# Attention's last rows on the whole TensorE array, and two small steps of other stages made on POOL

## The chip, the core and the metric

One core of a Trainium2 chip runs the whole program in one launch. The metric is device time in microseconds, the median of a few runs. TensorE (PE in the profile, with its weight loads as PEld) multiplies, VectorE (DVE), ScalarE (ACT) and GpSimd (POOL) do the elementwise work, and SyncE (SP) issues the DMAs.

## What is computed

Three layers follow each other: causal attention with a decay from the cumulated sums of `s`, an FFN whose activation is h cos h, and an RMS-normed gated FFN. The weights come as 64-bit floats.

```python
# attention: q, k, v (4, 8, 576, 64), s (4, 8, 576)
scores = q @ k.T / 8
cum = cumsum(maximum(s, 0))
bias = -(cum[:, None] - cum[None, :])
scores = where(causal, -1e9, scores + minimum(bias, 0))
attn = exp(scores - max(scores)); attn = attn / (sum(attn) + 1e-9)
x = attn @ v                      # -> (2304, 512)
# FFN 1: w_in (512, 2048), w_out (2048, 512)
h = x @ w_in;  x = (h * cos(h)) @ w_out
# FFN 2: w_gate, w_val (512, 1536), w_out (1536, 512)
xn = x / rms(x) * rms_g
out = (silu(xn @ w_gate) * (xn @ w_val)) @ w_out
```

## The kernel before

Attention works on 16 pairs of heads, one head in partitions 0 to 63, the other in 64 to 127. A pair's 576 rows are cut in parts: "a" (rows 0 to 255) and "b" (rows 256 to 575). Rows 256 to 383 and 384 to 511 are scored per head by `score` (L427, the product; L432, the decay added by another matmul). The last 64 rows of both heads share one tile of 128 partitions, called "p" (`score_p`): for each half of 288 keys, two matmuls of 64 contraction rows by 64 columns (L455) write head 0 to the upper and head 1 to the lower half of one PSUM bank, and one matmul over all 128 partitions (L456) adds the decay. A float32 matmul shows as two MATMULs in the trace, a transpose and a matmul of type fp32r as one. DVE adds the mask and takes the row minimum (L439, L459), ACT takes the exponential with its row sum `rs` (L467), `norm` makes 2 pi / (sum + 1e-9) as two small DVE steps (L475, L477) and scales the rows by it (L482 to L484, one of three engines). PE transposes the tiles against `ident` (L498), the result is copied to `P` (L284, L287), and `av` multiplies by V (L530): for part "b" five key tiles for two heads, the last of them 64 keys by the 64 last rows. V is padded with zeros to 640 rows and Q holds, behind row 512, the last rows of head 0 and of head 1 in columns of their own, with zeros in the other head's partitions.

FFN 1 runs 72 units of 24 + 12 matmuls (`gemm1` L630, `gemm2` L636), all of the full 128 x 128 shape, the first of them between attention's work. FFN 2 runs 72 units of 24 + 9 (the same lines, 384 columns a block). TensorE works in split single precision: each weight is a rounded part and its rest.

A weight chunk (`chunk`, 68 of them: 32 for FFN 1, 36 for FFN 2) is made from 64-bit floats, loaded to `raw` (3 buffers) as pairs of 32-bit words, the low word first. The high word times 2^-112 goes to `cv` (2 buffers) on POOL (L359) or ACT (L360). DVE then shifts it left by 3 (L362), adds the sign bit of the high word (L363) and the top 3 bits of the low word (L365). A copy (L284, L287 or L291) rounds it into the weight tile and a subtraction (L295 on DVE or L297 on POOL) makes the rest.

The order of all instructions of an engine is fixed when the program is built: `Plan.order` is a list scheduler that takes the ready step with the lowest due time on the engine that is free first, by the costs written beside each step, and, where a step may run on several engines, picks the one that its costs make earliest. An engine runs its list in order, so what stands at its head and waits holds up all behind it. A change of costs or of steps therefore moves others.

## Time and profile before

| | us |
|---|---|
| median of 3 runs | 1119.66 (1119.5 to 1120.15) |
| the profiled execution's own time | 1122.79 |
| its span, first to last instruction | 1121.0 |
| PE busy in it | 1091.6 |
| DVE, ACT, POOL busy | 567.0, 535.5, 139.8 |

Attention ends near 306 us. From there to about 600 us only FFN 1 runs, from about 600 to 716 us FFN 1's last units stand beside 30 of the weight chunks of FFN 2, and after that FFN 2 runs alone. The page's busy share of PE is not its share at full rate: the end of each matmul is modelled to overlap the next one's start, so a length of the timeline is to be read from start to next start. The granted clock of PE has two levels, 1.2 and 2.4 GHz. The page shows it at 7 tenths of the upper one in the first of its 40 slices and at 9 or more in all others; a window from 14 to 20 us has 0.50 of it, one from 612 to 616 us 0.83 and one from 616 to 620 us 0.75.

### The profile page before, as it was taken

The numbers are of one execution on the slowest core, as the hardware profiler recorded it, in microseconds if no ns is written. First come the engines' busy times: TensorE is split into PE (matmuls) and PEld (weight loads), VectorE is DVE, ScalarE is ACT, GpSimd is POOL, SyncE is SP. The second block draws the span as 40 slices with busy tenths as digits, with TensorE's granted clock in tenths as the row PEclk, the third lists the DMA queues.
The fourth block names the chain that finished last, engine by engine and source line by source line (L and its number), as shares of the span: only waits on it lengthen the run. The fifth ranks groups of instructions, "written<-read, shape, count | busy, mean of one in ns | idle before, by whom it ended". The sixth has DMA issues, their size and how long they took to land.

```text
span 1121.0 us, 16903 instructions
## 1 busy us (share of the span) xinstructions
PE 1091.6 (97%) x6538; PEld 933.7 (83%) x6538; DVE 567.0 (51%) x1296; ACT 535.5 (48%) x1113; POOL 139.8 (12%) x152
## 2 busy tenths in 40 slices
PE   8899999999999999999999899999999999999998
PEld 6457676676799999999998788899999999999997
DVE  7896999775464444534447989621221211211211
ACT  5889898998844444434435555321221211211111
POOL 3331244111020000000002332100000000000000
PEclk7999999999999999999999999999999999999999
DMA  6663676744293010000102446110010100100000
GB/s 197 226 203 127 214 271 220 228 133 135 77 379 115 19 38 20 20 23 16 38 20 78 157 118 208 56 57 1 3 55 1 57 1 1 43 1 1 29 1 29
DMA packets 51376, 101.27 MB, mean 90 GB/s; under 512 B 7520, under 2 KB 27488, under 8 KB 51296
## 3 DMA queue, kind: packets, MB, share of 16 engines
q1 hardware_dynamic: 51296, 100.19, 27.1%
q8 instruction: 51, 0.84, 0.3%
q14 instruction: 29, 0.24, 0.1%
HBM read 77.63 MB, written 22.54 MB: 89 GB/s over the span
## 4 chain that ended last, share of the span: by engine, by line
PE 54%; issue 25%; DVE 14%; DMA 3%; ACT 3%; POOL 1%; DVEq 0%; POOLq 0%; SPq 0%; ACTq 0%
PE bank L630 27%; PE bank L636 15%; PE bank L498 3%; PE bank L530 3%; DVE cv L363 3%; DVE cv L365 3%; PE bank L427 3%; DMA wr<-wo_d 2%; DVE cv L362 1%; DVE u L295 1%; DVE e L439 1%; PE bank L455 1%; PE bank L432 1%; DVE rn L475 1%; DMA raw<-in_w_gate_dram 1%
## 5 line engine op out<-in xcount | busy, mean ns | idle before, releaser
L636 PE MATMUL bank<-wr,g 128*128 128x512 f32 x996 | 248.6, 398 | 5.3 <-ACT g L284 5.3
L295 DVE TENSOR_TENSOR u<-bank,u 128x512 f32<-128x512 f32 (+1 forms) x144 | 89.8, 623 | 317.2 <-PE bank L630 238.9
L630 PE MATMUL bank<-xa,wi 128*128 128x256 f32 x1728 | 223.5, 284 | 1.6 <-DVE u L295 1.6
L630 PEld LDWEIGHTS bank<-xa,wi 128*128 128x128 f32 x1728 | 217.5, 191 | 8.4 <-DVE u L295 2.0
L636 PEld LDWEIGHTS bank<-wr,g 128*128 128x128 f32 x996 | 183.9, 190 | 42.9 <-ACT g L284 6.7
L284 ACT ACTIVATE g<-u 128x512 fp32r<-128x512 f32 (+1 forms) x131 | 75.4, 576 | 266.0 <-DVE u L295 266.0
L295 DVE TENSOR_TENSOR g<-u,g 128x512 fp32r<-128x512 f32 (+1 forms) x127 | 80.9, 637 | 70.0 <-ACT g L284 69.8
L630 PE MATMUL bank<-xb,wi 128*128 128x384 f32 x528 | 101.6, 337 | 0.0
L630 PEld LDWEIGHTS bank<-xb,wi 128*128 128x128 f32 x528 | 93.2, 188 | 1.6
L630 PE MATMUL bank<-xb,wr 128*128 128x384 f32 x480 | 92.5, 337 | 0.0
L295 DVE TENSOR_TENSOR u<-u,bank 128x512 f32<-128x512 int32 x72 | 49.4, 685 | 80.4 <-ACT u L740 79.2
L740 ACT ACTIVATE u<-bank,quarter 128x512 int32<-128x512 f32 x72 | 49.4, 686 | 83.7 <-PE bank L630 81.9
L630 PEld LDWEIGHTS bank<-xb,wr 128*128 128x128 f32 x480 | 85.1, 188 | 1.7
L467 ACT ACTIVATE e<-e,mn 128x128 f32<-128x128 f32 (+3 forms) x128 | 70.6, 555 | 13.9 <-DVE mn L439 13.5
L742 ACT ACTIVATE u<-u,half_pi 128x512 f32<-128x512 f32 x72 | 52.1, 724 | 38.5 <-DVE u L295 38.3
L636 PE MATMUL bank<-wi,g 128*128 128x512 f32 x270 | 67.0, 392 | 0.0
L822 ACT ACTIVATE u<-bank 128x384 f32<-128x384 f32 x72 | 35.3, 490 | 64.4 <-PE bank L630 56.3
L439 DVE CUSTOM_DVE_ANT_0 e<-bank,cm 128x128 f32<-128x128 f32 (+3 forms) x128 | 57.7, 484 | 15.4 <-PE bank L432 15.1
L636 PE MATMUL bank<-ws,g 128*128 128x512 f32 x246 | 64.5, 401 | 0.0
L359 POOL TENSOR_SCALAR cv<-raw 128x512 f32<-128x512 f32 x22 | 17.1, 777 | 348.2 <-DVE wi L295 277.6
L636 PEld LDWEIGHTS bank<-wi,g 128*128 128x128 f32 x270 | 50.3, 188 | 9.7 <-ACT g L284 0.3
L498 PE MATMUL bank<-ident,e 128*128 128x128 f32 x320 | 53.7, 287 | 3.9 <-DVE mn L439 3.4
(129 smaller groups left out, 1456.0 us busy)
## 6 DMA issues: line engine op xcount, KB each, us to landing
raw<-in_w_out_dram SPq DMA_DIRECT2D x28, 512.0 KB, 4.4
raw<-in_w_in_dram SPq DMA_DIRECT2D x16, 512.0 KB, 3.8
wo_d<-ws SPq DMA_DIRECT2D x16, 512.0 KB, 3.7
ws<-wo_d SPq DMA_DIRECT2D x16, 512.0 KB, 4.5
wr<-wo_d SPq DMA_DIRECT2D x16, 512.0 KB, 10.6
raw<-in_w_gate_dram SPq DMA_DIRECT2D x12, 512.0 KB, 3.8
raw<-in_w_val_dram SPq DMA_DIRECT2D x12, 512.0 KB, 3.7
qr<-in_q_dram SPq DMA_DIRECT2D x16, 320.0 KB, 4.5
```

The source lines that it names most:

```text
L284: alts.append(("ACT", (act_p if psum else act_s)(n), lambda: act.activation(o(), i(), AF.Copy, scale=scale)))
L295: alts = on("DVE", dve1(n), lambda: dve.tensor_tensor(out=o(), in0=a(), in1=b(), op=op))
L363: plan.op(on("DVE", dve1(512), lambda: dve.scalar_tensor_tensor(out=v(), in0=top(), scalar=-(2 ** 31), in1=v(), op0=ALU.bitwise_and, op1=A ...
L365: plan.op(on("DVE", dve1(512), lambda: dve.scalar_tensor_tensor(out=v(), in0=low(), scalar=29, in1=v(), op0=ALU.logical_shift_right, op1=A ...
L439: plan.op(on("DVE", dve1(w) + 17, lambda o=o, w=w, i=i, e=e: dve.tensor_tensor_reduce(out=Es[e]()[:, o:o + w], in0=Sp[e]()[:, o:o + w], in ...
L467: plan.op(on("ACT", act_s(w) + 187, lambda E=E, o=o, w=w, i=i: act.activation(E()[:, o:o + w], E()[:, o:o + w], AF.Exp, scale=-1.0, bias=s ...
L498: pe.transpose(tr()[:m, 128 * j:128 * j + 128], E[0]()[:, E[2] + c:E[2] + c + m], ident)
L630: pe.matmul(h, w[:, a, 128 * k:128 * k + 128], x[k // 2][:, k % 2, c, :blk], start=(n == 0), stop=(n == 11))
L636: pe.matmul(acc[t], g[a][:, 128 * t:128 * t + 128], w[:, c, :], start=(first and (a, c) == (0, 0)), stop=(last and (a, c) == (1, 0)))
L740: plan.op(on("ACT", act_p(512) + 93, lambda u=u, h=h: act.activation(u().bitcast(I32), h(), AF.Identity, bias=quarter)), [h], [u])
L742: plan.op(on("ACT", act_s(512) + 93, lambda u=u: act.activation(u(), u(), AF.Sin, scale=-TWO_PI, bias=half_pi)), [], [u], table="sin")
L822: plan.op(on("ACT", act_p(BLK2), lambda us=us, h=hs[0]: act.activation(us(), h()[:, :BLK2], AF.Silu)), [hs[0]], [u], table="silu")
```

## The change

Four edits, which leave the result what it was:

- `score_p` multiplies both heads at once. The Q columns 512 to 639 are block diagonal over the two heads, so one float32 matmul over 128 contraction rows and 128 columns gives what the two of 64 x 64 gave. Its cost in the plan falls.
- The tile "p" is 640 wide instead of 576, its 64 last columns are set to zero once by POOL, before the loads of `s`. The transpose of its last columns takes 128 instead of 64, the copy to `P` 128 partitions instead of 64, and the last key tile of `av` contracts over 128 rows, 64 of them zero.
- In `chunk`, POOL multiplies the high word in place by zero, which leaves its sign alone; DVE then ors the low word's top bits into it (L364 of the new code), and a second DVE step shifts `cv` by 3 and ors the two (L366). Three DVE steps become two, and a POOL step is added to each of the 68.
- The first small step of `norm` (L475, the sum plus 1e-9, times 2 pi) runs on POOL; 48 instructions leave DVE.

```diff
-           3: ring("e3", 2, [128, 512], F32, "att"), "p": ring("ep", 2, [128, S], F32, "att")}
+           3: ring("e3", 2, [128, 512], F32, "att"), "p": ring("ep", 2, [128, 640], F32, "att")}
...
-        plan.op(on("DVE", dve2(512), lambda: dve.tensor_scalar(out=v(), in0=v(), scalar1=3, scalar2=None, op0=ALU.logical_shift_left)), [], [g])
+
+        plan.op(on("POOL", pool1(512), lambda: pool.tensor_scalar(out=top().bitcast(F32), in0=top().bitcast(F32), scalar1=0.0, scalar2=1.0, op0=ALU.mult, op1=ALU.mult)), [], [raw])
         plan.op(on("DVE", dve1(512), lambda: dve.scalar_tensor_tensor(
-            out=v(), in0=top(), scalar=-(2 ** 31), in1=v(), op0=ALU.bitwise_and, op1=ALU.bitwise_or)), [raw], [g])
+            out=top(), in0=low(), scalar=29, in1=top(), op0=ALU.logical_shift_right, op1=ALU.bitwise_or)), [], [raw])
         plan.op(on("DVE", dve1(512), lambda: dve.scalar_tensor_tensor(
-            out=v(), in0=low(), scalar=29, in1=v(), op0=ALU.logical_shift_right, op1=ALU.bitwise_or)), [raw], [g])
+            out=v(), in0=v(), scalar=3, in1=top(), op0=ALU.logical_shift_left, op1=ALU.bitwise_or)), [raw], [g])
...
             def qk():
-                for e in range(2):
-                    hd, q0 = slice(64 * e, 64 * e + 64), 512 + 64 * e - run.qs.start
-                    pe.matmul(Sp()[hd, :288], run.q()[hd, q0:q0 + 64], run.k()[hd, gs], start=True, stop=False)
+                q0 = 512 - run.qs.start
+                pe.matmul(Sp()[:, :288], run.q()[:, q0:q0 + 128], run.k()[:, gs], start=True, stop=False)
                 pe.matmul(Sp()[:, :288], run.pk(), ds()[:, o + gs.start:o + gs.stop], start=False, stop=True)
-            plan.op(on("PE", 488 + 127 + 2 * SWITCH_PE, qk), [run.q, run.k, run.pk, (ds, o)], [Sp], rows=0.9)
+            plan.op(on("PE", 480 + 127 + SWITCH_PE, qk), [run.q, run.k, run.pk, (ds, o)], [Sp], rows=0.9)
...
-            plan.op(on("DVE", 204, lambda: dve.tensor_scalar(
+            plan.op(on("POOL", 204, lambda: pool.tensor_scalar(
...
-... + [("p", 512, 64)],
+... + [("p", 512, 128)],
...
-                out(lambda: P()[:64, 3, 0:64], lambda: tr()[:64, 384 + 64 * e:448 + 64 * e], 64)
+                out(lambda: P()[:, 3, 0:64], lambda: tr()[:, 384 + 64 * e:448 + 64 * e], 64)
...
-                    jobs.append((4, 64, 256, 320, [p[:64, 3, 0:64] for p in ps]))
+                    jobs.append((4, 128, 256, 320, [p[:, 3, 0:64] for p in ps]))
...
+    for b in (s_b, cum):
+        plan.op(on("POOL", 130, lambda b=b: pool.memset(b()[:, S:640], 0.0)), [], [(b, "pad")])
```

The plan is made anew from these steps. Over the whole program the built order differs in the counted steps above and in who takes a free step: of the subtractions that make a weight's rest POOL has 34 before and 26 now (L297), and DVE, which has 53 row scalings (L483) before, now has 70 plus 6 of "p" instead of 11.

PE, one pair in the middle of attention, where the profile of before shows 212 us. Before, two 64-row matmuls and L456 stand between transposes (L498):

```order
L498 MATMUL bank_152<-ident,e_169 128x128 x4
L455 MATMUL bank_149<-kr_156,qr_154 64x288 x2
L456 MATMUL bank_149<-ds_161,pk_158 128x288
L498 MATMUL bank_150<-ident,e_168 128x128 x4
L455 MATMUL bank_151<-kr_156,qr_154 64x288 x2
L456 MATMUL bank_151<-ds_161,pk_158 128x288
```

The same place of the change:

```order
L498 MATMUL bank_152<-ident,e_169 128x128 x4
L455 MATMUL bank_149<-kr_156,qr_154 128x288
L456 MATMUL bank_149<-ds_161,pk_158 128x288
L498 MATMUL bank_150<-ident,e_168 128x128 x4
L455 MATMUL bank_151<-kr_156,qr_154 128x288
L456 MATMUL bank_151<-ds_161,pk_158 128x288
```

The place stays between the same neighbours; two instructions of half shape became one of full shape. Of the 32 such places 29 stood behind a full-shape matmul, and 30 do now.

DVE in the later part of FFN 2's weight chunks. Before, a chunk is three steps (L362, L363, L365) and the subtraction (L295) that ends it, if POOL doesn't make that one; here the end of one chunk and the whole of the next, with a step of an FFN unit between:

```order
L295 TENSOR_TENSOR wr_3171<-cv_128,wr_3171 128x512
L362 TENSOR_SCALAR cv_129<-cv_129 128x512
L363 SCALAR_TENSOR_TENSOR cv_129<-raw_127,cv_129 128x512
L365 SCALAR_TENSOR_TENSOR cv_129<-raw_127,cv_129 128x512
L295 TENSOR_TENSOR u_132<-bank_152,u_132 128x384
L295 TENSOR_TENSOR wr_3175<-cv_129,wr_3175 128x512
```

The same part now:

```order
L295 TENSOR_TENSOR wr_3154<-cv_128,wr_3154 128x512
L364 SCALAR_TENSOR_TENSOR raw_126<-raw_126 128x512
L366 SCALAR_TENSOR_TENSOR cv_129<-cv_129,raw_126 128x512
L364 SCALAR_TENSOR_TENSOR raw_127<-raw_127 128x512
L295 TENSOR_TENSOR wr_3157<-cv_129,wr_3157 128x512
L366 SCALAR_TENSOR_TENSOR cv_128<-cv_128,raw_127 128x512
```

A chunk is two DVE steps, and the first of them reads what POOL made. POOL in that stretch before, between roundings (L291) and subtractions (L297):

```order
L291 TENSOR_SCALAR wi_115<-cv_129 128x512
L297 TENSOR_TENSOR wi_115<-cv_129,wi_115 128x512
L297 TENSOR_TENSOR wr_3142<-cv_128,wr_3142 128x512
L297 TENSOR_TENSOR wr_3156<-cv_128,wr_3156 128x512
L297 TENSOR_TENSOR wi_117<-cv_129,wi_117 128x512
```

and now, with the new sign step (L363) of each chunk between them:

```order
L363 TENSOR_SCALAR raw_127<-raw_127 128x512
L291 TENSOR_SCALAR wi_115<-cv_129 128x512
L297 TENSOR_TENSOR wi_115<-cv_129,wi_115 128x512
L363 TENSOR_SCALAR raw_125<-raw_125 128x512
L363 TENSOR_SCALAR raw_126<-raw_126 128x512
L297 TENSOR_TENSOR wr_3112<-cv_128,wr_3112 128x512
L363 TENSOR_SCALAR raw_127<-raw_127 128x512
```

The sign steps stand in one list with the rounding and the subtraction of earlier chunks, and a chunk's DVE steps come after its own.

## Rows read from the trace of the kernel before

**Rows 1.** The page, part 1: busy time, share of the span, instructions, of each engine.

```profile
PE 1091.6 (97%) x6538; PEld 933.7 (83%) x6538; DVE 567.0 (51%) x1296; ACT 535.5 (48%) x1113; POOL 139.8 (12%) x152
```

**Rows 2.** Four stretches: start:end, length, busy of PE, PEld, DVE, ACT, POOL; PEclk; DMA.

```profile
60.00:120.00 60.00, 59.13 (x424) 38.86 (x422) 46.93 (x149) 54.37 (x139) 13.79 (x18) 1.00 0.51 166
120.00:200.00 80.00, 76.83 (x528) 53.98 (x522) 77.38 (x194) 72.36 (x167) 32.35 (x34) 1.00 0.71 238
200.00:310.00 110.00, 109.90 (x784) 78.66 (x781) 64.46 (x217) 94.24 (x219) 12.98 (x16) 1.00 0.44 140
600.00:720.00 120.00, 109.85 (x604) 97.84 (x603) 107.46 (x177) 63.15 (x113) 40.91 (x34) 0.99 0.46 142
```

**Rows 3.** The chain that ended last, share of each stretch by line, same four stretches.

```profile
by line: PE bank L530 19.3%; PE bank L498 19.0%; PE bank L427 16.3%; PE bank L630 14.3%; PE bank L455 8.4%; PE bank L636 5.0%; PE bank L456 4.4%; PE bank L432 4.1%; DVE e L439 2.2%; DVE rn L475 1.9%; issue 1.8%; DVE cv L363 1.6%; DVE cv L36
...
by line: DVE cv L363 13.2%; DVE cv L365 13.1%; DVE e L439 8.7%; issue 7.5%; DMA raw<-in_w_out_dram 5.2%; DVE u L295 5.2%; DVE cv L362 4.5%; DVE e L483 4.1%; DVE rn L475 4.1%; DVE P L287 3.9%; PE bank L530 3.5%; DVE wi L295 2.4%; DVE ws L295
...
by line: PE bank L498 20.4%; PE bank L530 17.4%; PE bank L636 17.2%; PE bank L630 17.1%; PE bank L427 12.7%; PE bank L455 5.7%; PE bank L456 3.0%; PE bank L432 2.9%; PE bank L720 0.9%; DVE st L701 0.9%; ACT xo L696 0.6%; ACT P L284 0.4%; DV
...
by line: issue 221.4%; DVE cv L363 14.7%; DVE cv L365 13.4%; PE bank L630 12.6%; PE bank L636 10.7%; DVE cv L362 7.3%; DVE u L295 6.3%; DVE y L709 4.0%; DVE wr L295 2.9%; POOL wi L297 2.8%; ACT wr L284 2.6%; DVE wi L295 2.6%; DVE g L295 2.5
```

**Rows 4.** PE timeline around one score_p: start, length, engine, line, operation, shapes, count.

```profile
212.99 0.60 PE L498 MATMUL bank<-ident,e 128*128 128x128 f32 x4
213.52 0.70 PE L455 MATMUL bank<-kr,qr 64*64 64x288 f32 x4
214.16 0.40 PE L456 MATMUL bank<-ds,pk 128*128 128x288 f32 x1
214.39 1.00 PE L630 MATMUL bank<-xa,wi 128*128 128x256 f32 x7
```

**Rows 5.** PE timeline a little earlier: both PV steps and one transpose group.

```profile
197.67 2.45 PE L530 MATMUL bank<-P,vr 128*64 128x320 f32 x20 [0.22 <-ACT P L284]
200.05 0.55 PE L498 MATMUL bank<-ident,e 128*128 128x128 f32 x3
...
203.72 0.87 PE L530 MATMUL bank<-P,vr 128*64 128x256 f32 x8
204.52 1.66 PE L636 MATMUL bank<-ws,g 128*128 128x512 f32 x6
...
208.07 0.66 PE L498 MATMUL bank<-ident,ep 128*128 128x128 f32 x4
208.48 1.67 PE L630 MATMUL bank<-xa,wi 128*128 128x256 f32 x12
```

**Rows 6.** L362 alone in two of the stretches: start:end, length, DVE busy, count; PEclk; DMA.

```profile
120.00:200.00 80.00, 9.18 (x18) 1.00 0.71 238
600.00:720.00 120.00, 13.72 (x30) 0.99 0.46 142
```

**Rows 7.** Four lines on DVE and POOL: ns min/median/max of one, first and last start.

```profile
L362 DVE TENSOR_SCALAR cv<-cv x68: 412/421/1529, 15.5 to 712.8; 128x512 int32<-128x512 int32 x68
...
L475 DVE TENSOR_SCALAR rn<-rs x48: 150/170/1243, 14.1 to 297.0; 128x4 f32<-128x4 f32 x16, 128x3 f32<-128x3 f32 x16, 128x2 f32<-128x2 f32 x16
...
L359 POOL TENSOR_SCALAR cv<-raw x22: 644/670/1080, 28.5 to 657.6; 128x512 f32<-128x512 f32 x22
...
L297 POOL TENSOR_TENSOR wi<-cv,wi x18: 1267/1531/1764, 20.0 to 695.2; 128x512 fp32r<-128x512 f32 x18
```

**Rows 8.** Timelines near 600 us, DVE first, then POOL: start, length, line, operation.

```profile
599.92 0.55 DVE L295 TENSOR_TENSOR xc<-xr,xc 128x384 fp32r<-128x384 f32 x1
...
607.43 1.00 DVE L295 TENSOR_TENSOR xc<-xr,xc 128x384 fp32r<-128x384 f32 x1
...
610.03 1.25 DVE L704 SCALAR_TENSOR_TENSOR st<-st 128x2 f32<-128x2 f32 x1
...
607.04 0.97 POOL L359 TENSOR_SCALAR cv<-raw 128x512 f32<-128x512 f32 x1
609.85 1.41 POOL L297 TENSOR_TENSOR wi<-cv,wi 128x512 fp32r<-128x512 f32 x1 [1.83 <-ACT wi L284]
```

More of the change, by code (lines that the diff above doesn't have):

```diff
@@ L490, in tr @@
                 self.P[e] = p32_r.new()
-            srcs = {0: [((e, 0), 0, 128), ((e, 1), 0, 128), ((e, 1), 128, 128)], 1: [((e, 2), 128 * c, 128) for c in range(3)] + [("p", 512, 64)],
+            srcs = {0: [((e, 0), 0, 128), ((e, 1), 0, 128), ((e, 1), 128, 128)], 1: [((e, 2), 128 * c, 128) for c in range(3)] + [("p", 512, 128)],
                     2: [((e, 3), 128 * c, 128) for c in range(4)], 3: [("p", 128 * c, 128) for c in range(4)]}[i]
@@ L579, in attention_moe_moe @@
     s_b, cum = e_r["p"].new(), e_r["p"].new()
-    load(s_b, lambda: s, 294912, [], [s_b])
-    plan.op(on("DVE", dve2(S), lambda: dve.tensor_scalar(out=s_b(), in0=s_b(), scalar1=0.0, scalar2=None, op0=ALU.max)), [], [s_b])
+    for b in (s_b, cum):
+        plan.op(on("POOL", 130, lambda b=b: pool.memset(b()[:, S:640], 0.0)), [], [(b, "pad")])
+    load(lambda: s_b()[:, :S], lambda: s, 294912, [], [(s_b, 0)])
+    plan.op(on("DVE", dve2(S), lambda: dve.tensor_scalar(out=s_b()[:, :S], in0=s_b()[:, :S], scalar1=0.0, scalar2=None, op0=ALU.max)), [], [(s_b, 0)])
     plan.op(on("DVE", dve1(S), lambda: dve.tensor_tensor_scan(
-        out=cum(), data0=ones.to_broadcast([128, S]), data1=s_b(), initial=0.0, op0=ALU.mult, op1=ALU.add)), [s_b], [cum])
+        out=cum()[:, :S], data0=ones.to_broadcast([128, S]), data1=s_b()[:, :S], initial=0.0, op0=ALU.mult, op1=ALU.add)), [(s_b, 0)], [(cum, 0)])
     def less(b, o, w, mid, scale=8.0, **kw):
@@ L587, in less @@
         plan.op(on("DVE", dve2(w) + 61, lambda: dve.tensor_scalar(
-            out=b()[:, o:o + w], in0=cum()[:, :w], scalar1=c(), scalar2=scale, op0=ALU.subtract, op1=ALU.mult)), [cum], [(b, o)], **kw)
+            out=b()[:, o:o + w], in0=cum()[:, :w], scalar1=c(), scalar2=scale, op0=ALU.subtract, op1=ALU.mult)), [(cum, 0)], [(b, o)], **kw)
     for i, (t, mid) in enumerate(((0, 63), (1, 191), (2, 319), ("p", 543), (3, 447))):
```

## The prediction

> **What bounds the kernel now.** I read the busy times first, then the stretches, then the chain of waits in each, and last the timelines of the places that the change touches. PE is busy for 1091.6 of 1121.0 us [rows 1], but its busy time counts drains and overlaps, so the stretches say more. From 60 to 120 and from 200 to 310 us PE has next to no idle time (59.13 of 60, 109.90 of 110 us busy, [rows 2]) and the chain lies on PE's lines; L455 alone, the half-shape score of the last rows, holds 8.4% of the first (5.0 us) and 5.7% of the second (6.3 us) [rows 3]. These stretches are PE-led: a nanosecond less on PE there is one less in total. From 120 to 200 us DVE leads: 77.38 of 80 us busy [rows 2], with the weight chunks' lines L363, L365 and L362 and the small L475 on the chain [rows 3]; PE idles for 3 us. ACT, at 72.36 us, is close behind DVE. From 600 to 720 us DVE leads again (107.46 of 120 us, PE 109.85), and L362 is 7.3% of that stretch on the chain, 8.8 us [rows 2, 3]. The "issue" in that row is a wait that began long before the stretch. Elsewhere PE runs FFN units that the change doesn't touch.
>
> **The change part by part.** *The score on the full array.* From L455's start to the start of what follows L456 the trace has 213.52 to 214.39, 0.87 us [rows 4]. Entering the half shape costs too: four transposes take 0.53 us up to L455 (212.99 to 213.52) and 0.41 us up to a full-shape matmul (208.07 to 208.48) [rows 4, 5], so 0.12 us more. Together 0.99 us. The two heads already run side by side: four MATMULs of 288 columns take 0.64 us (213.52 to 214.16), two passes of 0.32 with their drain. The change makes two passes of 288 columns with the full shape. No float32 product of that shape and length is in attention; the nearest are the PV steps, two passes of 256 and two of 128 columns in 0.80 us (203.72 to 204.52), and 2432 columns of passes in 2.38 us (197.67 to 200.05) [rows 5], about 1.0 ns a column with all drains. So a pass is at most 0.30 us; with a drain of some 0.1 us taken off each PV step it is 0.25, which I take. L456 takes 0.23 us now (214.16 to 214.39) because its weights come behind a switch; twelve FFN matmuls of 256 columns take at most 1.67 us [rows 5], 0.14 each, so 288 columns in step take 0.15. After: 2 x 0.25 + 0.15 = 0.65 us, saving 0.34 a place; the bounds are 0.16 (0.30 a pass, L456 unchanged) and 0.38 (0.80 ns a column, so 0.23 a pass). Eighteen of the 32 places lie in the PE-led stretches (5.0 and 6.3 us of chain at 0.63 a place, eight and ten): **6.1 us**, from 2.9 to 6.8.
>
> The rows show two tiles side by side gaining nothing over one full pass: 0.32 us a pass against the 0.25 estimated. The Trainium skill's page "TensorEngine Tiling (Array Packing)", section "Theoretical Speedup", speaks against the edit: a small dimension of 64 or less promises up to 2x from tiles. Were that factor lost here, with passes of 0.50 us, a place would cost 1.15 us instead of 0.99, and the 18 places would lose 2.9 us instead of gaining 6.1. I don't expect it, since both heads fit in one pass.
>
> *The last PV tile and the transposes.* Part "b" has 1664 more columns of passes than part "a" and takes 1.58 us longer (2.38 against 0.80) [rows 5]. That is 0.95 ns a column with the switch in it; at 0.80 to 0.90 without, it is 0.08 to 0.25 us too much for the columns alone: its switch to the 64-row shape. I take 0.12, as the entry above. Ten of 16 part "b" steps are in PE-led stretches: **1.2 us** (0.8 to 2.5). Transposing 128 instead of 64 columns changes nothing: the spacing of transposes is 0.10 us [rows 5], and the copies to P have the same 64 columns on more partitions. The two memsets of the pads come before the loads and are hidden by the wait for `s`.
>
> *The weight chunks.* L362 goes, 421 ns alone [rows 7] and 0.51 us on average in the one DVE-led stretch (9.18 us for 18), 0.46 in the other (13.7 for 30) [rows 6]. What it holds of the chain is 3.6 us (4.5% of 80) and 8.8 us [rows 3]. Added is a POOL step like L359, 670 ns, up to 1080 [rows 7], which the chunk's first DVE step waits for; before, the chunks scaled on ACT needed no POOL at all. It costs DVE time as well: L295 on `xc` takes 0.55 us alone and 1.00 us when POOL's L359 runs beside it (607.43 against 607.04 to 608.01) [rows 8], 0.45 us lost to one POOL step. The other end is nothing, when DVE is idle or reads PSUM. I take 0.2, under the middle, because in the last third of FFN 2's chunks POOL has few subtractions and its sign steps run ahead of DVE. So the first stretch keeps 0.51 - 0.2 = 0.31 us of a 0.51 us step, the second 0.26 of 0.46: 2.2 of 3.6 us and 5.0 of 8.8.
>
> *L475 to POOL.* 48 DVE steps of 170 ns median [rows 7] go; on the chain they are 4.1% of 80 us, 3.3 us, and 1.1 us from 60 to 120 [rows 3]. DVE's L477 now waits for POOL, where a subtraction of 1531 ns [rows 7] may stand ahead. But before, L475 itself stood still beside such a subtraction (1243 ns at most, [rows 7]). I keep half of it where DVE leads, 1.6 us, and nothing elsewhere.
>
> These sum to 8.8 us. Against that stands the list order on POOL: a sign step behind a rounding and a subtraction waits 0.7 + 1.5 us, and DVE's L364 waits at the head of its list, with the h and g steps of an FFN unit queued behind it, and PE behind those. Of the weights' subtractions 26 stay on POOL; I charge two or three such waits, 2.8 us, and keep **6.0 us** (0 to 16). PE's own savings in these stretches count nothing while DVE leads.
>
> Sum: 6.1 + 1.2 + 6.0 = 13.3 us. The profiled execution took 1122.79 us, 1.8 over its span and 3.1 over the median; it would become 1109.5. From the median, 1119.66 - 13.3 gives **1106**.
>
> **The rivals.** *Both bounds fall.* If POOL's steps hide, DVE gives its 15.7 us (3.6, 8.8, 3.3), and in the DVE-led stretches PE, then next in line, has its 14 cheaper scores (4.8 us) to follow with. With 7.3 us from the PE-led ones at most 27.8 us, 1092; with some of it lost to ACT, 1095. For it: POOL is busy for a third of those stretches [rows 2]. Against: ACT is at 72 of 80 us.
>
> *PE's part alone.* The new POOL step and its waits eat all that DVE gained: 1119.66 - 7.3 = 1112.
>
> *Slower: POOL's step holds DVE.* If each sign step holds DVE for as long as the longer rows show, 0.97 us (607.04) [rows 8], the 48 chunks of the two DVE-led stretches lose 48 x (0.97 - 0.48) = 23.5 us, less 7.3: 1136. It decides from 0.48 + 7.3 / 48 = 0.63 us a chunk on; one step beside L359 lost 0.45, and a step of 2 columns beside a subtraction took 1.25 us (610.03) [rows 8], to the end of that one. For it: two POOL operations may follow each other. Against: L359 itself stretches to 1080 ns, so it is POOL that waits in part of the cases. The Trainium skill's page "SBUF — State Buffer", section "Who interferes with whom", has the rule behind this: of GpSimd and a VectorE step with two SBUF inputs the later one blocks until the first has ended. The rows at 607 and 610 us agree with it.
>
> *It doesn't do what it says.* If a full-shape pass with its weight load costs what the pair costs, and POOL eats the rest, the time stays, 1119.
>
> **How the numbers follow.** The forecast has 0.52 (1100 to 1111 alone), both bounds fall 0.20, PE's part alone 0.15, no effect 0.04, slower 0.09. The range leaves out the slower case, the no-effect case and the last of the lower one: 1094 to 1115. Faster by over 0.2% (2.2 us, about what a measurement here tells from nothing) is 0.52 + 0.20 + 0.15 = 0.87, same 0.04, slower 0.09.
>
> **What would show it.** In the trace of the changed kernel the step from the last transpose group to L456's successor should be some 0.35 us shorter, the stretch of pure attention work should end 6 to 12 us earlier, DVE's busy time from 600 to 720 us should fall by about 10 us, and POOL's total should rise by some 60 us (68 x 0.7 and 48 small ones). The prediction is wrong if DVE's L364 shows idle time behind POOL's L363 of more than 0.3 us a chunk, if L364 or L366 take much longer than L363 and L365 did, if the plan's new order puts an FFN unit behind a late chunk, or if PE loses its clock in a wait that wasn't there before.

## The result, and the profile after

The changed kernel takes 1110.26 us (1108.53 to 1112.65 in four runs, before 1119.91 beside it): 0.9913 of before, with a 95% interval of 0.9901 to 0.9925. That is 9.7 us less (8.4 to 11.1). The prediction said 1106, with a range of 1094 to 1115: the side and the range were right, and of the 13.3 us that it summed 9.7 came. The profiled execution took 1108.53 us, 1.7 under the median.

The page, busy times over the whole program (of before: [rows 1]):

```profile
PE 1078.3 (97%) x6474; PEld 938.8 (85%) x6474; DVE 547.5 (49%) x1209; ACT 529.0 (48%) x1098; POOL 186.3 (17%) x256
```

PE is 13.3 us shorter, DVE 19.5, and POOL 46.5 longer. A part of PE's 13.3 is its clock at the start (last section), so that it equals the prediction's sum is chance. The span fell by 14.2 us (1121.0 to 1106.8), so PE's idle time, where DVE's relief would show, hardly moved: 29.4 us before, 28.5 now. Four stretches, as in [rows 2] (start:end, length, busy of PE, PEld, DVE, ACT, POOL; granted clock; DMA). The last starts 10 us earlier than there, since the same work does:

```profile
60.00:120.00 60.00, 57.53 (x413) 42.92 (x410) 48.85 (x128) 52.43 (x125) 27.61 (x40) 1.00 0.60 198
120.00:200.00 80.00, 77.64 (x525) 56.09 (x525) 72.92 (x184) 72.25 (x167) 45.20 (x59) 1.00 0.70 231
200.00:310.00 110.00, 110.00 (x789) 86.50 (x788) 61.23 (x197) 90.92 (x211) 16.40 (x32) 1.00 0.50 165
590.00:710.00 120.00, 112.02 (x618) 100.63 (x617) 101.13 (x156) 62.84 (x111) 48.86 (x54) 0.99 0.46 142
```

From 200 to 310 us PE is as full as it was. From 60 to 120 us it now idles for 2.5 us instead of 0.9. In the last stretch DVE fell from 107.46 to 101.13 us of 120, yet PE gained only 2.2 us of work. The chain that ended last, by line, from 120 to 200 and from 590 to 710 us (of before: [rows 3]):

```profile
by line: PE bank L638 10.9%; PE bank L498 9.1%; issue 8.2%; PE bank L428 7.0%; DMA raw<-in_w_out_dram 6.4%; ACT e L467 6.1%; PE bank L530 5.8%; DVE e L483 5.7%; DVE raw L364 5.7%; DVE cv L366 4.2%; DVE ep L459 2.3%; ACT ws L284 2.1%; POOL w
by line: issue 19.9%; DVE raw L364 14.1%; DVE cv L366 12.2%; POOL raw L363 7.5%; ACT cv L360 5.9%; DVE wr L295 4.9%; ACT wr L284 4.1%; DVE u L295 3.6%; DVE g L295 3.6%; PE bank L632 3.2%; POOL wr L297 2.5%; DVE wi L295 2.4%; POOL cv L359 2.
```

From 120 to 200 us the chunk's DVE lines went from 31% of the chain to 10%, and PE leads again. In the last stretch L362 with its 7.3% is gone, and POOL's L363 stands there with 7.5%, 9.0 us of 120: the new step took the dropped one's place on the chain.

The new score, PE's timeline around two places (start, length, line, shapes, count; of before: [rows 4]):

```profile
205.84 0.60 PE L498 MATMUL bank<-ident,e 128*128 128x128 f32 x4
206.28 0.65 PE L455 MATMUL bank<-kr,qr 128*128 128x288 f32 x2
206.55 0.51 PE L456 MATMUL bank<-ds,pk 128*128 128x288 f32 x1
206.90 0.60 PE L498 MATMUL bank<-ident,e 128*128 128x128 f32 x4
```

From start to start a transpose group takes 0.44 us, L455 0.27 and L456 0.35, 1.06 us together. Before it was 0.53, 0.64 and 0.23, 1.40 us [rows 4]. A place saves 0.34 us. Over all 32 places the medians are 0.63 and 0.24 us before and 0.27 and 0.35 now.

POOL's sign step, and who waits for it (count, ns min/median/max; then who waited, us in total and times):

```profile
L363 POOL TENSOR_SCALAR raw<-raw x68: 647/672/1199, 21.5 to 699.2; 128x512 f32<-128x512 f32 x68
...
who waited for it (us, times):
  DVE raw L364: 10.1, 16
```

Its length is that of L359 in [rows 7]; its mean is 765 ns, 52.0 us in all. DVE stands idle before L364 for 10.1 us in 16 cases, which is 0.15 us a chunk.

### The profile page after: what moved, and what is told of

Same layout as the page of the kernel before. It is cut to its first block, busy times and chain, and to the rows that moved or that the text cites. A ratio compares the mean times of both kernels' runs of the same rounds, so it can differ in the third digit from the quotient of the medians.

```text
span 1106.8 us, 16861 instructions
## 1 busy us (share of the span) xinstructions
PE 1078.3 (97%) x6474; PEld 938.8 (85%) x6474; DVE 547.5 (49%) x1209; ACT 529.0 (48%) x1098; POOL 186.3 (17%) x256
## 3 DMA queue, kind: packets, MB, share of 16 engines
q1 hardware_dynamic: 51296, 100.19, 27.5%
## 4 chain that ended last, share of the span: by engine, by line
PE 79%; DVE 10%; issue 4%; ACT 3%; POOL 3%; DMA 1%; DVEq 0%; POOLq 0%; ACTq 0%
PE bank L632 40%; PE bank L638 27%; PE bank L498 4%; PE bank L530 3%; PE bank L428 3%; DVE raw L364 2%; DVE cv L366 2%; POOL raw L363 1%; DVE e L483 1%; PE bank L455 1%; ACT cv L360 1%; PE bank L433 1%; ACT e L467 1%; DVE e L440 1%; DVE u L295 1%
## 5 line engine op out<-in xcount | busy, mean ns | idle before, releaser
L295 DVE TENSOR_TENSOR u<-bank,u 128x512 f32<-128x512 f32 (+1 forms) x144 | 89.7, 623 | 313.7 <-PE bank L632 235.0
L295 DVE TENSOR_TENSOR g<-u,g 128x512 fp32r<-128x512 f32 (+1 forms) x127 | 82.5, 650 | 67.8 <-ACT g L284 67.8
L295 DVE TENSOR_TENSOR u<-u,bank 128x512 f32<-128x512 int32 x72 | 49.3, 685 | 79.1 <-ACT u L742 77.4
L291 POOL TENSOR_SCALAR g<-u 128x512 fp32r<-128x512 f32 (+1 forms) x14 | 9.2, 657 | 340.0 <-DVE u L295 340.0
L359 POOL TENSOR_SCALAR cv<-raw 128x512 f32<-128x512 f32 x20 | 15.0, 749 | 293.4 <-DVE wi L295 254.3
L363 POOL TENSOR_SCALAR raw<-raw 128x512 f32<-128x512 f32 x68 | 52.0, 765 | 68.8 <-ACT cv L360 66.5
## 6 DMA issues: line engine op xcount, KB each, us to landing
wr<-wo_d SPq DMA_DIRECT2D x16, 512.0 KB, 10.2
```

Of the source, the lines that this page charges most:

```text
L295: alts = on("DVE", dve1(n), lambda: dve.tensor_tensor(out=o(), in0=a(), in1=b(), op=op))
L363: plan.op(on("POOL", pool1(512), lambda: pool.tensor_scalar(out=top().bitcast(F32), in0=top().bitcast(F32), scalar1=0.0, scalar2=1.0, op0= ...
```

## The experiments

**Theory:** PE's cheaper instructions bring their time in full, and the POOL edits little, because the sign step comes onto the chunk's own chain with its whole length. **Rivals:** the POOL edits bring the prediction's 6 us; or the time comes from the new order that the changed costs make, not from the instructions. Medians of four to eleven runs of each, and the ratio to before (1120.0 to 1120.4 us beside them):

| kernel | us | ratio, 95% interval |
|---|---|---|
| PE's part alone | 1115.05 | 0.9956 (0.9944 to 0.9968) |
| both POOL edits alone | 1116.07 | 0.9962 (0.9948 to 0.9976) |
| chunk edit alone | 1124.07 | 1.0029 (1.0019 to 1.0039) |
| norm's step alone | 1118.20 | 0.9987 (0.9978 to 0.9996) |
| new order, old PE instructions | 1114.23 | 0.9950 (0.9938 to 0.9962) |
| change without the chunk edit | 1113.07 | 0.9933 (0.9921 to 0.9946) |
| change, chunk edit in FFN 2 only | 1107.82 | 0.9886 (0.9871 to 0.9901) |
| change, sign step on 8 columns | 1097.05 | 0.9797 (0.9776 to 0.9818) |
| change, sign step made twice | 1141.96 | 1.0194 (1.0179 to 1.0208) |
| FFN 2 only, sign on ACT or POOL | 1103.22 | 0.9855 (0.9838 to 0.9871) |
| all chunks, sign on ACT or POOL | 1106.43 | 0.9878 (0.9861 to 0.9895) |
| FFN 2 only, sign on ACT | 1106.96 | 0.9881 (0.9867 to 0.9895) |

### PE's part alone

Against before:

```diff
-                for e in range(2):
-                    hd, q0 = slice(64 * e, 64 * e + 64), 512 + 64 * e - run.qs.start
-                    pe.matmul(Sp()[hd, :288], run.q()[hd, q0:q0 + 64], run.k()[hd, gs], start=True, stop=False)
+                q0 = 512 - run.qs.start
+                pe.matmul(Sp()[:, :288], run.q()[:, q0:q0 + 128], run.k()[:, gs], start=True, stop=False)
...
-                    jobs.append((4, 64, 256, 320, [p[:64, 3, 0:64] for p in ps]))
+                    jobs.append((4, 128, 256, 320, [p[:, 3, 0:64] for p in ps]))
```

> The kernel before with PE's part of the change alone: the last rows' score as one 128-row product, the pads, the 128-column transpose and the full last PV tile; the weight chunks and norm's first small step stay on DVE. Theory (PE's savings carry nearly the whole gain; the POOL edits give back most of what they take from DVE): 1110 to 1113 us, 7 to 10 below before and at most 3 above the whole change. Rival (each part gains about half): 1113 us or more, and the POOL edits alone bring 4 us or more. In both, a score place (from the first L455 to the start of what follows L456) is 0.34 us shorter and the end of attention's work comes 7 us earlier or more.

It took 1115.05 us, 5.3 less than before (3.6 to 6.3): less than the theory's 7, and a little over half of the gain. With the 4.3 us of both POOL edits alone (below) the rival of this expectation holds: each part gives about half. The same stretch from 60 to 120 us, and what PE waited for in it (us in total, times, longest):

```profile
60.00:120.00 60.00, 56.50 (x400) 40.55 (x399) 50.69 (x148) 53.87 (x128) 16.34 (x20) 1.00 0.60 196
```

```profile
PE bank L497 <- DVE mn L439: 2.3, 2, 1.6
```

PE idles for 3.5 us of it, 0.9 before [rows 2]. Part of what the cheaper score saves there PE spends waiting for DVE's row minima.

### New order, old PE instructions

Against the changed kernel; the plan's costs, the transposes and the copies to P stay the changed ones:

```diff
-                q0 = 512 - run.qs.start
-                pe.matmul(Sp()[:, :288], run.q()[:, q0:q0 + 128], run.k()[:, gs], start=True, stop=False)
+                for e in range(2):
+                    hd, q0 = slice(64 * e, 64 * e + 64), 512 + 64 * e - run.qs.start
+                    pe.matmul(Sp()[hd, :288], run.q()[hd, q0:q0 + 64], run.k()[hd, gs], start=True, stop=False)
...
-                    jobs.append((4, 128, 256, 320, [p[:, 3, 0:64] for p in ps]))
+                    jobs.append((4, 64, 256, 320, [p[:64, 3, 0:64] for p in ps]))
```

> The changed kernel's plan and instruction order, but with the instructions of before in two places: two 64 x 64 score products and the 64-row last PV tile. So it has the new order and all the POOL edits without PE's cheaper instructions. Theory (what PE saves is the instructions' own time, not the new order): 7 to 13 us above the whole change, 1117 to 1123. Rival (the lower costs in the plan gave a better order, and that is where the time came from): less than 4 us above it, 1110 to 1114.

1114.23 us, 4.0 above the whole change: between the two by the medians, nearer to the rival. Both kernels run one order, so the same matmul can be compared in the two profiled executions. The starts of some of FFN 1's 1728 first-product matmuls, read from the timelines:

| matmul | changed, us | old instructions, us |
|---|---|---|
| 1 | 80.3 | 79.2 |
| 169 | 182.2 | 184.0 |
| 313 | 287.8 | 293.6 |
| 361 | 302.4 | 308.4 |
| 1728 | 634.9 | 640.9 |
| end of span | 1106.8 | 1112.4 |

The changed kernel is 1.1 us late at the first of them and 6.0 ahead at the 361st, and stays so: 7.1 us, all of it within attention. The lead grows by some 0.35 us at each score place. Ahead of the first the changed kernel had a lead too, 1.3 us at 44 us, and lost it. PE then waited longer for DVE's row minima (first the changed kernel, then the old instructions):

```profile
47.81 0.81 PE L498 MATMUL bank<-ident,e 128*128 128x128 f32 x3 [2.85 <-DVE mn L440]
47.44 0.52 PE L499 MATMUL bank<-ident,e 128*128 128x128 f32 x3 [1.16 <-DVE mn L440]
```

From 47.9 to 51.3 us its granted clock was at 0.50 of the upper level, where the other kernel's stayed at 1.00, which cost 1.5 us more. So the instructions themselves are worth some 7 us from 80 us on. That speaks for the theory, though the times do not reach its 7: two of the four executions of the changed kernel had a lower mean clock (0.990 and 0.989, with 1111.61 and 1112.65 us) than the other two (0.995 and 0.994, with 1108.53 and 1108.9), and those two lie 5.7 and 5.3 us under the old instructions' median. The order by itself (1116.07 for both POOL edits in the old order, 1114.23 in the new) is not told apart from nothing.

### Both POOL edits, the chunk edit, norm's step

Against before, the chunk edit and norm's step; the three kernels have both, the first, and the second:

```diff
-        plan.op(on("DVE", dve2(512), lambda: dve.tensor_scalar(out=v(), in0=v(), scalar1=3, scalar2=None, op0=ALU.logical_shift_left)), [], [g])
+        plan.op(on("POOL", pool1(512), lambda: pool.tensor_scalar(out=top().bitcast(F32), in0=top().bitcast(F32), scalar1=0.0, scalar2=1.0, op0=ALU.mult, op1=ALU.mult)), [], [raw])
...
-            plan.op(on("DVE", 204, lambda: dve.tensor_scalar(
+            plan.op(on("POOL", 204, lambda: pool.tensor_scalar(
```

> The kernel before with the POOL edits alone: sign step of each weight chunk and norm's first small step on POOL; PE's work stays. Theory (POOL's sign step takes the place on the chain that the dropped DVE step had): 1116 to 1120 us, with DVE's busy time about 20 us lower and POOL's some 50 us higher. Rival (DVE relief counts where DVE leads, the prediction's 6 us): 1112 to 1115 us.

> The kernel before with the chunk edit alone (POOL sign step and two DVE steps in place of three); norm's small step stays on DVE. Theory: within 2 us of before, 1118 to 1122, since of the 12.4 us that the dropped step had on the chain the POOL step takes about as much. Rival (the chunk edit is worth its terms, about 4 to 7 us): 1112 to 1116. If it comes out slower than 1122, norm's move carries what gain there is in the POOL part.

> The kernel before with norm's first small step on POOL and nothing else changed. Theory (the parts of the change add up, so norm's move is worth what the two POOL edits together have over the chunk edit alone, 1116.1 against 1124.1): 1111 to 1114 us. Rival (norm's move is worth little by itself, as the 1.6 us of the prediction say, and the chunk edit alone came out bad by its order): 1117 to 1121 us.

Both together gain 4.3 us (2.7 to 5.8), at the lower end of the theory's times and not clear of the rival's. The chunk edit alone loses 3.7 us (2.1 to 4.4), where "within 2 us" was expected and the rival said a gain of 4 to 7; norm's step alone gains 2.1 us (0.4 to 2.5), so that the two add up, as the third expectation's theory has it, falls: +3.7 and -2.1 would be 1.6 us lost, not 4.3 gained. Where the chunk edit alone lost can be seen, if not why the plan came out so: PE in two stretches of its trace, then the same with both edits.

```profile
60.00:70.00 10.00, 7.33 (x50) 4.10 (x50) 7.06 (x18) 8.02 (x20) 5.89 (x8) 1.00 0.75 253
70.00:80.00 10.00, 7.19 (x39) 4.73 (x41) 7.48 (x24) 6.14 (x22) 2.90 (x3) 0.83 0.50 157
```

```profile
60.00:70.00 10.00, 8.86 (x61) 5.37 (x59) 8.05 (x22) 8.26 (x20) 6.66 (x9) 1.00 0.57 186
70.00:80.00 10.00, 9.03 (x62) 5.39 (x62) 7.12 (x25) 8.73 (x30) 3.20 (x6) 1.00 0.80 273
```

PE is idle for 5.5 of these 20 us and its clock falls to 0.83 in the second half; with both edits it is idle for 2.1 and holds its clock. In the chunk-alone kernel DVE waits there with norm's L476 at the head of its list until ACT's exponentials are done (4.0 us in four cases from 40 to 125 us). That norm's step on POOL lifts just this wait is argued from one look, not shown. The loss lies within attention: from the 601st of FFN 1's first products on, the chunk edit alone gains as the other kernels with it do (next table).

### The change without the chunk edit, and with it in FFN 2 only

Against the changed kernel: the first has the three old DVE steps in all 68 chunks, the second in FFN 1's 32. The second's edit, without the old steps that `old` chooses:

```diff
-    def chunk(src, w):
+    def chunk(src, w, old=False):
...
-        w1[f] = chunk(w_in[f], wi_r.new(f))
+        w1[f] = chunk(w_in[f], wi_r.new(f), True)
...
-        w2[0, f] = chunk(w_out[f], ws_r.new())
+        w2[0, f] = chunk(w_out[f], ws_r.new(), True)
```

> The whole change without the chunk edit: PE's part and norm's step on POOL, three DVE steps a chunk as before. Theory (the chunk edit loses time, some 4 us): 1105 to 1108 us, below the whole change. Rival (with norm's step on POOL the chunk edit does bring its gain): 1112 us or more.

> The whole change, but the chunk edit only for the 36 chunks of FFN 2; the 32 of FFN 1, which are made beside attention, keep their three DVE steps. Theory (the sign step pays where DVE alone leads, from 580 to 720 us, and loses beside attention, where POOL has other steps that DVE waits for): 1104 to 1108 us. Rival (the two places don't differ): between the whole change and the one without the chunk edit.

Without the chunk edit 1113.07 us: the theory that it loses time in the whole change falls. By the medians it brings 2.8 us, with intervals that just overlap (0.9921 to 0.9946 and 0.9901 to 0.9925). With PE's part (5.3) and norm's (2.1) that makes 10.2, against 9.7 measured for the whole. With the edit in FFN 2's chunks only it is 1107.82 us, 5.2 below none, which is shown, and 2.4 below all, with intervals that touch (0.9871 to 0.9901 and 0.9901 to 0.9925). So the opening theory that the POOL edits bring little falls: they bring 4.3 us alone and 4.8 on top of PE's part. The version with FFN 2's chunks only is the fastest of those that compute the reference's result.

Where the time goes can be read more closely than the medians allow. By the 601st of FFN 1's first products PE has done the same work in every kernel, all of attention in it, and has the same work left. One profiled execution of each:

| kernel | sign steps on | 601st starts, us | from there to the end, us |
|---|---|---|---|
| before | none | 371.6 | 749.4 |
| PE's part alone | none | 364.2 | 749.0 |
| norm's step alone | none | 366.8 | 749.1 |
| change without the chunk edit | none | 361.9 | 749.0 |
| change | POOL, 68 | 359.9 | 746.9 |
| new order, old PE instructions | POOL, 68 | 365.9 | 746.6 |
| both POOL edits alone | POOL, 68 | 370.3 | 747.2 |
| chunk edit alone | POOL, 68 | 375.6 | 747.1 |
| change, chunk edit in FFN 2 only | POOL, 36 | 357.8 | 747.3 |
| change, sign step on 8 columns | POOL, 68 | 361.2 | 738.6 |
| change, sign step made twice | POOL, 68 | 380.4 | 760.9 |
| FFN 2 only, sign on ACT or POOL | both, 36 | 356.8 | 743.0 |
| all chunks, sign on ACT or POOL | both, 68 | 360.1 | 744.2 |
| FFN 2 only, sign on ACT | ACT, 36 | 361.3 | 744.4 |

The last column holds 30 of FFN 2's 36 chunks and nothing of attention or of PE's start, and kernels with the same chunk steps agree in it to 0.7 us. There the chunk edit is worth some 2.1 us in every kernel that has it whole on POOL. The rest of a kernel's time comes before. Without the edit, with it in all chunks, and in FFN 2's, from the 601st on:

```profile
361.90:1110.90 749.00, 732.84 (x4137) 672.52 (x4135) 291.66 (x514) 246.14 (x438) 50.57 (x44) 1.00 0.13 40
359.90:1106.80 746.90, 733.89 (x4137) 674.06 (x4135) 285.58 (x494) 246.15 (x437) 60.06 (x65) 1.00 0.13 41
357.80:1105.10 747.30, 735.02 (x4137) 675.13 (x4135) 285.04 (x494) 246.29 (x437) 60.32 (x65) 1.00 0.13 40
```

DVE gives 6.1 us, and the time falls by 2.1. The version with FFN 2's chunks only is in its theory's range, but not for the theory's reason: of the 5.8 us that it is ahead of the kernel without the edit (spans 1105.1 and 1110.9), 4.1 stand at the 601st matmul, when only six of its 36 sign steps have run. The two run alike, within 0.1 us, up to 189 us. From there to 345 us PE idles for 3.7 us without the edit and for 0.5 with it; the longest of these waits, 1.7 us for a tile `u` of DVE, comes behind attention's end. The built order changed there, and its part isn't told apart from the six steps' own. That FFN 1's 32 chunks lose beside attention isn't shown either: the change is 2.1 us behind this version at the 601st matmul, level with it at 43 us and 1.3 behind at 53 us, and between these its clock was at 1.2 GHz (from 47.9 us, as above) and the other's was not. That leaves 0.8 us.

### The sign step shorter, and twice

Against the changed kernel, one edit for each kernel:

```diff
-... lambda: pool.tensor_scalar(out=top().bitcast(F32), in0=top().bitcast(F32), scalar1=0.0, ...
+... lambda: pool.tensor_scalar(out=top().bitcast(F32)[:, :8], in0=top().bitcast(F32)[:, :8], scalar1=0.0, ...
```

```diff
-... lambda: pool.tensor_scalar(out=top().bitcast(F32), in0=top().bitcast(F32), scalar1=0.0, scalar2=1.0, op0=ALU.mult, op1=ALU.mult) ...
+... lambda: [pool.tensor_scalar(out=top().bitcast(F32), in0=top().bitcast(F32), scalar1=0.0, scalar2=1.0, op0=ALU.mult, op1=ALU.mult) for _ in range(2)][-1] ...
```

> The whole change, with the sign step run on 8 of the 512 columns of each chunk; the other columns keep their high word's bits, so the weights are not the reference's. Plan, order and waits are those of the change; only the step's length and its hold on the port go, some 0.5 us each. Theory (the step's own length is what the chain pays, 7.5% of the stretch from 590 to 710 us): 1102 to 1106 us. Rival (what costs is the place in POOL's list, behind roundings and subtractions): within 2 us of the whole change, 1108.5 to 1112.

> The whole change with each sign step made twice in a row on POOL; the result and the order of all engines stay. It prices the step from the other side than the run on 8 columns. Theory (the step's length is on the chain and on DVE's port; cutting it by 0.45 us each gave 13 us): 68 more steps of 0.7 us give 15 to 25 us, 1125 to 1135. Rival (the gain of the short step came from its strange data, or one step more hides): 1110 to 1115.

The short step gives 1097.05 us, 13.2 below the change and further than the theory's 1102; the doubled one 1141.96, 31.7 above it and further than 1135. The order of every engine is that of the change in both, so these are prices of the step alone. L364's idle time behind L363 (us, times), first the short step, then the doubled:

```profile
  POOL raw L363: 2.2, 5
```

```profile
  POOL raw L363: 32.9, 40
```

DVE's wait goes from 2.2 us in 5 cases over 10.1 in 16 to 32.9 in 40. DVE's own steps get longer as well: it is busy for 534.1 us with the short step, 547.5 in the change, 557.1 with the doubled one. The first difference is 13.4 us over 68 steps, 0.20 us a step, so waiting and holding cost about the same. From the 601st matmul on, short and doubled (the change above):

```profile
361.20:1099.80 738.60, 731.29 (x4137) 672.98 (x4135) 276.81 (x494) 246.29 (x437) 47.71 (x65) 1.00 0.13 41
380.40:1141.20 760.80, 740.72 (x4137) 678.19 (x4135) 289.41 (x494) 246.26 (x437) 85.26 (x95) 0.99 0.13 40
```

That is 8.3 us less and 14.0 more. Beside attention the step is paid for too: at the same matmuls the short step's kernel gains 3.5 us on the change between 74 and 204 us, and the doubled one loses 13.5 between 107 and 196 us, a part of it to its clock, which was at 1.2 GHz from 168.3 to 175.1 us. The chain from 590 to 710 us, short and doubled (whose late work starts some 20 us later, so that the window holds less of it):

```profile
by line: PE bank L632 31.1%; PE bank L638 21.3%; issue 7.3%; DVE raw L364 7.0%; DVE cv L366 5.0%; DMA raw<-in_w_gate_dram 3.6%; DVE u L295 3.5%; DVE wi L295 3.0%; DVE st L706 1.9%; DVE y L711 1.9%; DVE g L295 1.8%; ACT cv L360 1.6%; POOL cv
```

```profile
by line: POOL raw L363 16.8%; issue 12.9%; DVE raw L364 11.0%; DVE cv L366 8.9%; PE bank L632 7.6%; PE bank L638 7.0%; ACT cv L360 3.9%; DVE u L295 3.5%; DVE g L295 3.2%; DMA raw<-in_w_val_dram 2.9%; POOL cv L359 2.7%; DVE wi L295 2.4%; POO
```

With the short step half of the stretch is PE's own time; in the change it was 7.5% POOL and 26% the chunk's two DVE steps, and doubled POOL's step is the longest entry. POOL's busy time falls by 30.7 us (186.3 to 155.6) for 13.2 us of time, and rises by 54.5 us (to 240.8) for 31.7. The second is worth more by the us; there PE's clock falls as well, to a mean of 0.983 in the profiled execution, from 0.995 in the change's.

### The sign step on ACT

Against the version with FFN 2's chunks only, the step may be planned on either engine (or, in the third kernel, has ACT alone); the second kernel is the whole change with this line:

```diff
-        plan.op(on("POOL", pool1(512), lambda: pool.tensor_scalar(out=top().bitcast(F32), in0=top().bitcast(F32), scalar1=0.0, scalar2=1.0, op0=ALU.mult, op1=ALU.mult)), [], [raw])
+        plan.op(on("POOL", pool1(512), lambda: pool.tensor_scalar(out=top().bitcast(F32), in0=top().bitcast(F32), scalar1=0.0, scalar2=1.0, op0=ALU.mult, op1=ALU.mult)) + [("ACT", act_s(512), lambda: act.activation(top().bitcast(F32), top().bitcast(F32), AF.Copy, scale=0.0))], [], [raw])
```

> The whole change with the chunk edit for FFN 2's 36 chunks only, and the sign step free to be planned on ACT or POOL (12 go to ACT, 24 stay). Theory (what costs is POOL's time and its hold on DVE, 0.19 us of DVE a step): 2 to 4 us below the version with all 36 on POOL, 1104 to 1106. Rival (the step's place in the chunk's chain costs, on whatever engine it stands): 1106 to 1109.

> The whole change, all 68 chunks, the sign step free to be planned on ACT or POOL (26 go to ACT, 42 stay). Theory (POOL's time and hold cost): 4 to 6 us below the whole change, 1104 to 1106. Rival (ACT, at 72 of 80 us from 120 to 200 us, becomes the bound beside attention): 1109 to 1113.

> As the version with the chunk edit for FFN 2's 36 chunks only, but all 36 sign steps on ACT. Theory (without POOL's hold and queue DVE gets its 0.5 us a chunk back, and ACT, at 71 of 140 us from 580 to 720, has room): 1101 to 1105 us. Rival (ACT's copies and silu steps then wait, or the step's own length in the chunk's chain is what counts): 1106 to 1110.

On ACT this product doesn't leave what the next step needs, so the weights of these three kernels are not the reference's; they are read for time alone. All 36 on ACT is worth nothing against all on POOL by the medians (1106.96 and 1107.82), which is the rival's range. What waits for the step there (first FFN 2 with ACT alone, then with both):

```profile
L370 ACT ACTIVATE raw<-raw x36: 656/672/710, 197.7 to 700.3; 128x512 f32<-128x512 f32 x36
...
  DVE raw L371: 6.7, 11
```

```profile
L370 POOL TENSOR_SCALAR raw<-raw x24: 643/674/1216, 186.2 to 687.7; 128x512 f32<-128x512 f32 x24
...
L370 ACT ACTIVATE raw<-raw x12: 661/686/701, 586.6 to 691.0; 128x512 f32<-128x512 f32 x12
...
  DVE raw L371: 3.9, 6
```

The step is as long on ACT, and DVE waits 6.7 us for it, where it waited 4.9 us for POOL's in the version with FFN 2's chunks only. Shared between the two engines the wait is 3.9 us and the time 1103.22, a little under the theory's 1104 to 1106. With all chunks and a free choice it is 1106.43, 3.8 below the change, where 4 to 6 was expected. From the 601st matmul on, ACT alone takes 744.4 us, 2.9 less than POOL in the same 36 chunks:

```profile
361.30:1105.70 744.40, 734.30 (x4137) 674.00 (x4135) 279.65 (x492) 260.81 (x462) 44.11 (x42) 1.00 0.13 41
```

DVE is busy for 279.65 us there and not 285.04: what POOL's step took from it comes back, though it waits longer. What is gained so was lost before the 601st matmul, 3.5 us, most of it from 320 to 345 us: PE idles there for 2.5 us, as it does without the edit, and not at all with POOL's 36 steps. So it is neither POOL's hold alone nor the chain alone, and the place of the medians hangs on the built order around attention's end as well.

## Why the prediction was right, and where its sum was off

**The score place: right.** 0.34 us a place predicted, 0.34 measured. The split was not the predicted one: L455 takes 0.27 us from start to start instead of 0.50, L456 0.35 instead of 0.15 (more without the switch ahead of it than its 0.23 with it), and the entry is 0.09 cheaper instead of 0.12. That these errors cancel is luck; the reason, that both heads fit in one full-shape product, was right. The Trainium skill's page "TensorEngine Tiling (Array Packing)", section "Theoretical Speedup", promises up to 2x from tiles for a dimension of 64 or less. The trace doesn't bear this out here: the two products side by side take 0.64 us, and one full-shape product for both heads, with zeros in half of its operand, 0.27.

**The last PV tile: right.** 0.12 us a step predicted. From start to next start part "b"'s twenty MATMULs take 2.206 us now and took 2.353 (medians), 0.15 less.

**PE-led stretches, 7.3 us: right for the instructions, too high for the whole.** The same order with old and new instructions shows 6.3 us in the two stretches (2.0 from 60 to 120 us, 4.3 from 200 to 310) and 1.3 in the one between, where the prediction had none. PE's part alone gave 5.3 in the medians, 2.0 short. From 60 to 120 us PE had only 0.9 us of idle time in the kernel before; with its cheaper work it idles for 3.5, most of it behind DVE's row minima, and the lead made before 44 us went the same way. A stretch at 59.13 of 60 us is PE-led only as far as the next engine allows.

**The POOL edits, 6.0 us: too large by 1.2 to 1.7.** Norm's step, 1.6 predicted, is worth 2.1 alone (0.4 to 2.5). The chunk edit was put at 4.4 us; it brings 2.8. The step of the prediction that went wrong is the charge for the wait: two or three waits behind a rounding and a subtraction were charged, 2.8 us, while L364 waited 16 times, 10.1 us, 5.0 of them from the 601st matmul on. Of the 16 sign steps waited for only one came straight from a subtraction; seven had first waited for ACT's scaling of the chunk, and five followed POOL's own scaling. So DVE waits for the step's own length, which lies in the chunk's chain between the scaling and DVE's first step (7.5% of 590 to 710 us).

The 0.2 us of DVE time for each sign step is what the short step shows on average, but in the late stretch it is 0.29 (285.58 less 276.81 us, over 30 steps). With 0.17 us of wait (5.0 over 30) that makes 0.46, as much as L362 took there [rows 6]; that 2.1 us are left all the same, this account does not explain. The late stretch was put at 5.0 us before the charge. If all of the 2.8 is charged there, its 2.2 meets the 2.1 measured, by errors that cancel. For the chunks beside attention, put at 2.2, the whole change is 2.0 us ahead of the kernel without the edit at the 601st matmul, of which the built order's part stays open. The 3.6 us that are missing from the whole sum are split between PE's part and the POOL edits only as well as the intervals allow, which are some 1.4 us to either side for each. One meeting of the two engines in the trace of the changed kernel, near 613 us, DVE first, then POOL:

```profile
613.64 0.69 DVE L364 SCALAR_TENSOR_TENSOR raw<-raw 128x512 int32<-128x512 int32 x1
614.36 1.03 DVE L366 SCALAR_TENSOR_TENSOR cv<-cv,raw 128x512 int32<-128x512 int32 x1
...
613.65 1.20 POOL L363 TENSOR_SCALAR raw<-raw 128x512 f32<-128x512 f32 x1 [0.52 <-ACT cv L360]
```

POOL's step, 0.67 us alone, takes 1.20 beside L364, and L366 after it 1.03 instead of its median 0.69: DVE lost 0.34 us, POOL 0.53. That a step of GpSimd and a VectorE step with two SBUF inputs get in each other's way is what the Trainium skill's page "SBUF — State Buffer", section "Who interferes with whom", states, and the trace agrees.

**The rivals.** "Slower: POOL's step holds DVE" had the mechanism and the point from which it decides; the doubled step reaches it (1141.96, where it said 1136 for 0.97 us a chunk), the real one stays under it. A sign step costs DVE 0.20 us of busy time and 0.15 of wait in the change, 0.34 and 0.48 doubled (557.1 less 534.1, and 32.9, over 68); the rival decides from 0.63 on. "Both bounds fall" (1092 to 1095) is nearly what a sign step of almost no length gives, 1097.05: the room was there, and the step used it up. "PE's part alone" (1112) came nearer to 1110.26 than the forecast, but not by its reason: the POOL edits do gain, 4.3 us alone, and PE's part gave 5.3 where it had 7.3.

**The signs that were named.** The score place shorter by 0.35 us: seen. Attention's end 6 to 12 us earlier: its last PV matmul starts at 293.7 us and before at 305.4, 11.7 earlier, of which a part is the clock at the start; against the old instructions in the same order it is 6.0. DVE 10 us lower in the late stretch: 6.3. POOL 60 us higher: 46.5, since other steps left it. L364's idle time stayed under 0.3 us a chunk, at 0.15; the bound was set too high to catch what happened.

## What to carry to other kernels

Two half-array products that fill different quarters of the array are worth joining into one full-shape product with a block-diagonal operand, and the price is read from start to start over the whole place, with the switch on either side. A step that moves from a full engine to an idle one still lies in the chain of its own data: add its whole length there, and what it takes from the full engine while it runs. To price such a step, make it shorter and make it twice in the built order. And compare kernels from one matmul on to the end, where they have the same work left: what the start and the built order scatter over the medians falls out, and a gain shows in which stretch it was made.

## What the runs showed of the chip beyond that

Executions differ by when PE's clock rises at the start. The stretch from 18 to 28 us in the profiled execution of before, then of the change (the granted clock is the third number from the right):

```profile
18.00:28.00 10.00, 9.42 (x43) 6.53 (x42) 6.78 (x22) 7.39 (x23) 3.50 (x4) 0.52 0.47 141
```

```profile
18.00:28.00 10.00, 8.84 (x64) 6.33 (x66) 6.42 (x25) 9.85 (x30) 4.31 (x8) 1.00 0.35 127
```

PE was busy for 10.05 and 9.91 of the first 14 us, then both fell to 1.2 GHz; the change's was back at 2.4 GHz at 17.2 us, before's only at 27.5, with PE busy for 9.42 of the 10 us shown. The kernel with the short sign step, which has the change's order, was back only at 27.1 us. That the executions of one kernel scatter by this is not shown, since each kernel was profiled once; their mean clocks scatter (0.989 to 0.995 in the change's four, with 1112.65 to 1108.53 us). The profiled executions of before and of the change differ by 14.2 us of span where the medians differ by 9.7, so traces are compared by how a lead grows from one matmul to a later one, not by their ends.
